# A reordered plan in a fused attention and token/channel mixer: five product tiles, a two-part split of the token result, and two more places for the token products

## The chip, the cores and the metric

The kernel runs on one core of one Trainium2 chip. The metric is the device time of one execution in microseconds (us). Engines are called as the profile calls them: PE (matrix products), PEld (its weight loads), DVE (vector), ACT (scalar), POOL (it issues the DMAs that accumulate) and SP (it issues most other DMAs).

## The reference

```python
def _attn_ref(x, weight_gen):                 # x: 8 x 4096 x 192, weight_gen: 8 x 4096 x 8 heads x 7
    w = softmax(weight_gen, axis=-1)
    out = np.einsum('bshk,bskhg->bshg', w, x_unf)   # 7 taps of the 6 rows before and the row itself
def _moe_ref(x, w_tok1, w_tok2, w_ch1, w_ch2):
    xt = x.transpose(0, 2, 1)
    h = np.maximum(xt @ w_tok1, 0.0) @ w_tok2       # over the 4096 tokens, 256 wide
    u = x + h.transpose(0, 2, 1)
    h2 = np.maximum(u @ w_ch1, 0.0) @ w_ch2         # over the 192 channels, 1536 wide
    return (u + h2).astype(np.float32)
```

The reference's weights are float64; the kernel receives them as such and turns each into float32 words on the chip ("conversion").

## The kernel before

The work is cut into 64 chunks of 512 tokens, `g` = 0 to 63, eight to a batch element. A prologue does the attention of the first eight chunks and their token-1 products. After it, one chunk of the main loop has four kinds of PE work:

- **channel 1** (`ph`, L573): six products of 18 matmuls, from the token result in two parts, `u_hi` and `u_lo`, each a single buffer;
- **channel 2** (`acc`, L591): six products `p` = 0 to 5 of 10 matmuls, from `h`, which ACT (L579) and DVE (L580) make of `ph` (four buffers of `h`). `p` = 4 and 5 read the last third of `w2s`;
- **token 2** (`up`, L524): 10 matmuls that give the token result of chunk g + 1. ACT first writes the residual into its bank (L518, the seed). Afterwards ACT and DVE copy the sum into `uf` (L531, L532, L536), and `u_parts` splits it: `u_hi` by L546 to L552 on ACT, `u_lo` by L548 and L549 on DVE and L553 to L555 on ACT;
- **token 1** (`th`, L507 in the first two batch elements, L490 and L492 later): adds one chunk of the next batch element into a running sum of eight. The eighth sum, through a relu, makes `h1`, without which token 2 of the next batch element can't start.

`ph`, `up` and `th` share three PSUM buffers in turn (`ps_w`). The fourth `ph` of a chunk so waits until the first has been read by L580, and the seed of an `up` that follows six `ph` waits for the fourth L580.

Beside this, DVE forms the attention of later chunks: 7 products (L211) and 3 additions (L225) for each chunk, two chunks at a time, through the tiles `pr` (four), whose sums POOL adds to `xa` by an accumulating DMA (L229). DVE and ACT also convert the rest of the weights (ACT L155 to L157, then DVE L159 to L161, then the split L166, L167), through `val` tiles of which three serve at a time. Token-1 weights of batch element 1 come back from DRAM into `val` tiles too (`load_w1`). At a chunk's end DVE turns the output (L645, L646, L648) and ACT copies it out in 12 pieces (L655).

What stands where on ACT and DVE is no fixed order. While the program is built, `pump` keeps a list of chains (attention, transposes, softmax, conversions, parts of u, stores) and a clock per engine of its own (`at`), and emits the next item of a chain when by that clock it fits before the next thing that PE needs. The constants near L677 (`SLACK_M`, `LATER` and so on) and the gates in the chains decide it. `picks` chooses whether token 1 or token 2 comes at the head of channel 2 or before `p` = 3. On the chip each engine then runs its list strictly in that order.

Of the kernel before, what the change touches and what calls it, by code (L numbers as in the profile page):

```python
# [12 lines left out]
F32 = mybir.dt.float32  # L13
# [8 lines left out]
def mixer_kernel(ctx: ExitStack, tc: tile.TileContext, x, wg, wt1, wt2, wc1, wc2, out):  # L22
    nc = tc.nc
    B, S, D = x.shape
# [20 lines left out]
    XA = 4  # L45
    PR = 4
    FT = NCH - 2
# [9 lines left out]

    ident = const.tile([P, P], F32, name="ident")
    make_identity(nc, ident)
    below = const.tile([P, 1], F32, name="below")  # L60
# [85 lines left out]
    def convert(raw, n, out):  # L146

        yield "gate", 0, lambda: state["vals"] < 2
        state["vals"] += 1
        v = val_tile()[:, 0:n]  # L150
        out.append(v)
        bits = v.bitcast(U32)
        low, high = raw[:, 0:n, 0], raw[:, 0:n, 1]
        act, stt = nc.scalar.activation, nc.vector.scalar_tensor_tensor
        yield "s", 950, lambda: act(v, high.bitcast(F32), AF.Abs)  # L155
        yield "s", 1050, lambda: act(v, v, AF.Sign, bias=below[:, 0:1])
        yield "s", 950, lambda: act(v, v, AF.Relu, scale=LOW30)  # L157
# [3 lines left out]
        yield "v", cost, lambda: stt(bits, high, 0xC0000000, bits, op0=ALU.bitwise_and, op1=ALU.bitwise_or)  # L161
# [98 lines left out]
    def two_parts(m):  # L260

        yield "gate", 0, lambda: state["token1"] >= m - 1

# [137 lines left out]
    def convert_w2(i):  # L401
        out = []
        yield from convert(rawt.pop(("w2", i)), KR * N, out)
        yield "n", 0, lambda: raw_free(tag_of["w2", i])
        yield "gate", 0, lambda: state["token2"] >= i - 1
        v, = out
        t = p1.tile([P, 2, KR * N], F32R, tag="w2", name="w2")
        yield from split(t[:, 0], t[:, 1], v)

        def last():  # L410
            state["vals"] -= 1
            w2t[i] = t
            nc.gpsimd.dma_start(s3[i], t.rearrange("p l n -> p (l n)").bitcast(F32))
        yield "n", 0, last
# [26 lines left out]
    def convert_channel(which, n, pool=None):  # L441
# [15 lines left out]
        def last():  # L457
            state["vals"] -= 1
            done.add((which, n))
        yield "n", 0, last  # L460
# [14 lines left out]
    def token1(m):  # L475
# [62 lines left out]
    def u_parts(m):  # L538
# [4 lines left out]
        f, act, dve = lo.bitcast(F32), nc.scalar.copy, nc.vector.tensor_sub  # L543
        yield "gate", 0, lambda: state["channel1"] >= m
        yield "w", 0, lambda: free["parts"]
        yield "u", 620, lambda: act(hi[:, 0], ua)  # L546
        yield "u", 620, lambda: act(hi[c, 2], uc[c])
        yield "v", 610, lambda: dve(lo[:, 0], ua, hi[:, 0].bitcast(F32))  # L548
        yield "v", 610, lambda: dve(lo[c, 2], uc[c], hi[c, 2].bitcast(F32))  # L549
        yield "u", 620, lambda: act(hi[c, 1], ua[e])  # L550
        yield "u", 620, lambda: act(hi[e, 1], ua[c])
        yield "u", 620, lambda: act(hi[e, 2], uc[c])  # L552
        yield "u", 620, lambda: act(lo[c, 1], f[e, 0])  # L553
        yield "u", 620, lambda: act(lo[e, 1], f[c, 0])  # L554
        yield "u", 620, lambda: act(lo[e, 2], f[c, 2])  # L555

        def last():
            ut[m] = hi, lo
            free["u"] = at["act"] + HOP
        yield "n", 0, last  # L560

# [134 lines left out]
    w_at, h1_at, h1s_at = deque([0.0] * 3), {0: 0.0}, [0.0]  # L696
    free = {"acc": 0.0, "u": 0.0, "t": 0.0, "parts": 0.0, "xh": 0.0}
    pr_free = deque([0.0] * PR)
# [87 lines left out]
    def next_lo():  # L786
# [7 lines left out]
             "summed": NCH - 1, "turned": FT - 1, "parts": NCH - 1, "kept": FT - 1, "stored": -1, "out": -1,  # L794
             "done": NCH - 1, "w1": NCH, "channel1": 0, "rest": 0}

# [53 lines left out]
    with tc.tile_pool(name="pro", bufs=1) as pro, \  # L850
            tc.tile_pool(name="ps_pro", bufs=1, space=bass.MemoryType.PSUM) as ps_pro:
        warm = pro.tile([P, 1], F32, name="warm")
        nc.scalar.activation(warm, ident[:, 0:1], AF.Exp)
# [7 lines left out]
        def start(items):  # L861

            items = iter(items)
            for _ in range(4):
                next(items)[2]()
            return items
# [73 lines left out]
    run(u_parts(0))  # L940
    free["u"] = 0.0
# [4 lines left out]
    at["dve"], at["act"] = 3500, 1500  # L946
    add_chain(load_w1(NCH))
    state["token2"] = 0

# [8 lines left out]
    def do_token1(it, m, t):  # L958
# [19 lines left out]
    def do_token2(it, m, t):  # L978
# [5 lines left out]
        w_at.append(t)  # L984
        chains.insert(3, Chain(u_parts(m), t, ("u", m)))
        state["token2"] = m
# [12 lines left out]
    def picks(g, soon, most):  # L999

        two = token2_ready(g + 1, soon)
        if two:
# [9 lines left out]
    for g in range(NG):  # L1012
        phs, kept = {}, {}
        soon = ((convert_w2, 1),) if g == 0 else ()
        for p in range(NP):
# [7 lines left out]
            if p < HB:  # L1023
                take_h(g, p, phs[p])
                w_at.append(on("dve", LOW, on("act", TOP, end)))
                if p == 0:
                    h_at = w_at[-1]
                if p == HB - 2:
# [10 lines left out]
        for p in range(NP):  # L1039
            if p == NP // 2:  # L1040
# [13 lines left out]
            on("pe", C2, free["acc"] if p == 0 else 0.0, h_at)  # L1054
            state["rest"] -= C2
            if p + HB < NP:
# [5 lines left out]
                take_h(g, p + HB, phs[p + HB])  # L1062
                h_at = on("dve", LOW, on("act", TOP, at["pe"]))
                if kept[p] in w_at:
                    w_at[w_at.index(kept[p])] = h_at
                if last:
                    picked += list(it)
                    h_at = 0.0
        pump(at["pe"] + SLACK_M)
# [45 lines left out]
```

## Time and profile before

| | |
|---|---|
| median of 3 runs | 2135.1 us (2129.74 to 2135.57) |
| the profiled execution | 2131.6 us, its span 2129.8 us |
| ACT busy | 68% of the span |
| POOL busy | 7% of the span |
| DMA moved | 363.82 MB, mean 171 GB/s |

A profile row of a group gives the line, engine, operation, the tiles, the count, then the busy time in us and the mean of one in ns, then the idle time of the engine before them with what ended it. A row of the timeline gives the start in us, the duration, the same names, and in brackets the idle time just before. A float32 product stands twice in the trace (16 rows for the 8 matmuls of a `th`).

### The profile page before, as it was taken

The page shows a single profiled execution, that of the slowest core. Times are in us where ns is not written, and L with a number is a line of the kernel's source. Part 1 is how long each engine was busy: PE and PEld are TensorE (multiplying, and loading weights), DVE is VectorE, ACT ScalarE, POOL GpSimd, SP SyncE. Part 2 cuts the span into 40 slices and gives each one's busy share as a digit, 9 for nine tenths or more (in the row PEclk, how much of TensorE's full clock was granted, in tenths as well). Part 3 has the DMA queues.
Part 4 walks back from the last instruction along what each step waited for, and adds up shares of the span by engine and source line. Part 5 has one row for each costly group of instructions (what it writes and reads, how often), then busy time and mean ns, then how long its engine had stood idle before and what let it go on. Part 6 is the DMA issues. An engine that isn't in the chain of part 4 may idle for free.

```text
span 2129.8 us, 32140 instructions
## 1 busy us (share of the span) xinstructions
PE 2085.4 (98%) x12766; PEld 1691.5 (79%) x12766; DVE 1538.5 (72%) x1760; ACT 1440.3 (68%) x2226; POOL 158.2 (7%) x194
## 2 busy tenths in 40 slices
PE   7989899999999999999999999999999999999998
PEld 5767788787878888888888888888888888888887
DVE  8978988788887777777777877777787765343433
ACT  5568666667766766676676677667666766766665
POOL 0001111000100010000000010000100000000000
PEclk9999999999999999999999999999999999999999
DMA  8666757878687667566766756676665655321221
GB/s 279 225 213 171 207 147 210 253 200 230 185 234 202 189 172 190 150 182 181 196 189 173 200 156 174 171 202 193 173 194 149 181 163 148 89 66 45 64 63 23
DMA packets 166198, 363.82 MB, mean 171 GB/s; under 512 B 16552, under 2 KB 105896, under 8 KB 150688
## 3 DMA queue, kind: packets, MB, share of 16 engines
q1 hardware_dynamic: 139808, 285.74, 42.8%
q0 software_dynamic: 25344, 74.46, 17.8%
q8 instruction: 100, 1.64, 0.3%
q10 hardware_dynamic: 896, 1.57, 0.2%
q14 instruction: 50, 0.41, 0.1%
HBM read 225.13 MB, written 70.52 MB: 139 GB/s over the span
## 4 chain that ended last, share of the span: by engine, by line
PE 82%; DVE 10%; ACT 4%; DMA 3%; issue 2%; POOL 0%; SPq 0%; ACTq 0%; DVEq 0%; POOLq 0%
PE acc L591 36%; PE ph L573 33%; PE up L524 7%; PE th L490 3%; DVE h L580 2%; DVE pr L211 2%; PE th L492 1%; DVE prk L327 1%; DMA raw<-in_moe_w_tok_dram 1%; PE th L507 1%; DMA xt<-in_x_dram 1%; DMA xa<-pr 1%; DVE val L160 1%; DVE val L159 1%; DVE pr L225 1%
## 5 line engine op out<-in xcount | busy, mean ns | idle before, releaser
L591 PE MATMUL acc<-h,w2s 128*128 128x512 f32 x3800 | 884.5, 390 | 2.5 <-DVE w2s L454 2.5
L591 PEld LDWEIGHTS acc<-h,w2s 128*128 128x128 f32 x3800 | 709.2, 188 | 148.9 <-DVE w2s L454 2.9
L579 ACT ACTIVATE h<-ph 128x1024 fp32r<-128x1024 f32 x384 | 394.4, 1027 | 396.2 <-PE ph L573 340.1
L580 DVE SCALAR_TENSOR_TENSOR h<-ph,h 128x1024 fp32r<-128x1024 f32 x384 | 467.1, 1217 | 121.3 <-ACT h L579 120.8
L573 PE MATMUL ph<-u_hi,w_hi 64*128 64x512 f32 x2304 | 343.5, 396 | 13.8 <-ACT u_hi L550 5.8
L573 PE MATMUL ph<-u_hi,w_lo 64*128 64x512 f32 x2304 | 332.9, 389 | 0.0
L573 PE MATMUL ph<-u_lo,w_hi 64*128 64x512 f32 x2304 | 332.4, 388 | 0.0
L211 DVE TENSOR_TENSOR pr<-xt,wg 128x768 f32<-128x768 f32 x336 | 314.0, 949 | 8.9 <-DMA xa<-pr 8.1
L573 PEld LDWEIGHTS ph<-u_hi,w_hi 64*128 64x128 f32 x2304 | 216.8, 185 | 82.8 <-issue 21.5
L573 PEld LDWEIGHTS ph<-u_hi,w_lo 64*128 64x128 f32 x2304 | 221.9, 185 | 47.3
L573 PEld LDWEIGHTS ph<-u_lo,w_hi 64*128 64x128 f32 x2304 | 221.8, 185 | 47.4 <-ACT u_lo L554 0.6
L229 POOL DMA_DIRECT2D xa<-pr x168 | 144.6, 861 | 1439.0 <-DVE pr L225 1236.9
L536 DVE TENSOR_TENSOR uf<-up,uf 64x512 f32<-64x512 f32 x63 | 43.0, 682 | 243.2 <-ACT uf L532 243.2
L655 ACT COPY out_tile<-oa 32x256 f32<-32x256 f32 x504 | 203.5, 404 | 7.8
L524 PE MATMUL up<-w,h 128*128 128x512 f32 x630 | 161.7, 402 | 5.9 <-ACT up L518 5.9
L225 DVE TENSOR_TENSOR pr<-pr 128x768 f32<-128x768 f32 x168 | 160.3, 954 | 3.7
L524 PEld LDWEIGHTS up<-w,h 128*128 128x128 f32 x630 | 113.8, 188 | 48.8 <-ACT up L518 16.2
L518 ACT COPY up<-xb 128x1024 f32<-128x1024 f32 x63 | 64.0, 1016 | 84.6 <-DVE h L580 81.5
L490 PE MATMUL th<-xh,w 128*128 128x384 f32 x384 | 112.5, 358 | 1.1 <-ACT th L483 1.1
L655 ACT COPY out_tile<-oc 32x256 f32<-32x256 f32 x252 | 101.6, 403 | 11.0 <-DVE oc L648 6.8
L269 DVE TENSOR_TENSOR xh<-xa,xh 128x768 fp32r<-128x768 f32 x48 | 45.9, 955 | 73.3 <-ACT xh L266 73.3
L492 PE MATMUL th<-xh,w 128*128 128x192 f32 x384 | 96.2, 250 | 0.0
(86 smaller groups left out, 1717.8 us busy)
## 6 DMA issues: line engine op xcount, KB each, us to landing
w<-s SPq DMA_DIRECT2D x96, 1024.0 KB, 5.3
xa<-pr POOLq DMA_DIRECT2D x168, 384.0 KB, 4.9
xt<-in_x_dram SPq DMA_DIRECT2D x56, 960.0 KB, 9.8
out_dram<-out_tile SPq DMA_DIRECT2D x128, 192.0 KB, 3.2
xs<-t SPq DMA_DIRECT2D x58, 384.0 KB, 4.6
xb<-xs SPq DMA_DIRECT2D x348, 64.0 KB, 5.0
raw<-in_moe_w_tok_dram SPq DMA_DIRECT2D x16, 1024.0 KB, 6.0
s<-w POOLq DMA_DIRECT2D x8, 1024.0 KB, 5.3
```

The lines of the kernel that those rows point to most:

```text
L211: nc.vector.tensor_mul(t.rearrange("p t (h g) -> p (t h) g", h=H).rearrange("p (o n) g -> p o n g", o=1), x_k, w)
L225: nc.vector.tensor_add(sums[m], sums[m], prt.pop(m))
L229: nc.gpsimd.dma_start(xat[m].rearrange("p t d -> p (t d)"), sums[m].rearrange("p t d -> p (t d)"), accum_op=ALU.add)
L490: nc.tensor.matmul(th[:, r, 0:2 * D], w[:, c, 0, rs], xh[:, c, :], start=i + c == 0, stop=False, skip_group_check=True)
L492: nc.tensor.matmul(th[:, r, 0:D], w[:, c, 1, rs], xh[:, c, 0:D], start=False, stop=c == CT - 1, skip_group_check=True)
L518: nc.scalar.copy(up.rearrange("p k (n b c) -> p (k n) c b", c=CT, b=Q), xb.rearrange("p k (n c b) -> p (k n) c b", c=CT, b=Q))
L524: nc.tensor.matmul(up[:, n, :], h1[:, k, d], w[:, l, k * N:(k + 1) * N], start=k == 0 and j == 0 and not seeded, stop=k == KR - 1 and j == ...
L573: nc.tensor.matmul(ph[:, j, :], w[rows, k, p * P:(p + 1) * P], u[rows, k], start=n == 0, stop=n == len(steps) - 1)
L579: nc.scalar.activation(h[:, :, 0, :], ph, AF.Relu)
L580: nc.vector.scalar_tensor_tensor(h[:, :, 1, :], ph, 0.0, h[:, :, 0, :].bitcast(F32), op0=ALU.max, op1=ALU.subtract)
L591: nc.tensor.matmul(acc[:, n, :], w2s[:, f, d], h[:, j, l, :], start=False, stop=f == NF - 1 and i == len(steps) - 1, skip_group_check=True)
L655: nc.scalar.copy(dst, src[to:to + Q].rearrange("p (n e d) -> p n e d", n=2, d=Q)[:, n])
```

## The change

`PR` becomes 5; `val` tiles become four after the prologue (with a wait in the plan's clock), and `ident` moves to the prologue's pool. The parts of u become two chains: one with the first two copies and all of `u_lo`, one with the three other copies of `u_hi`. Token-1 weights are fetched two chunks ahead from the start. The gate that let a chunk's sum count as ready only in turn goes for batch element 1. Channel 2 may have token 1 or token 2 also before its last product, and a token 1 that is behind (`ready[0][0] < g + NCH`, from g = 9) comes ahead of token 2 at its head. The wait for the last third of `w2s` moves in the plan from `p` = 3 to `p` = 4. Two matmuls of 128 columns are added at chunk 16's token 1. The plan keeps one due time per `h` and has other values of `LATER` and `SLACK_M`.

```diff
-    PR = 4
+    PR = 5
-        pool = pro if pro is not None and n % 6 >= 3 else p1
-        return pool.tile([P, NV], F32, tag="val", name="val", bufs=3)
+        pool = pro if pro is not None and n % 6 >= 4 else p1
+        return pool.tile([P, NV], F32, tag="val", name="val", bufs=2 if pool is pro else 4)
+        yield "w", 0, lambda: free["val"]
...
-        yield "gate", 0, lambda: state["token1"] >= m - 1
+        if m // NCH >= F1:
+            yield "gate", 0, lambda: state["token1"] >= m - 1
...
+                if m == F1 * NCH:
+                    nc.tensor.matmul(th[:, r, 2 * D:], w[:, CT - 1, 0, rs], xh[:, 0, 0:N - 2 * D],
+                                     start=False, stop=True, skip_group_check=True)
...
+        def first():
+            yield from begin()
+            yield "u", 620, lambda: act(hi[:, 0], ua)
+            yield "u", 620, lambda: act(hi[c, 2], uc[c])
+            yield "n", 0, lambda: taken.update(at=at["act"] + HOP)
+            yield "v", 610, lambda: dve(lo[:, 0], ua, hi[:, 0].bitcast(F32))
+            yield "v", 610, lambda: dve(lo[c, 2], uc[c], hi[c, 2].bitcast(F32))
+            yield "u", 620, lambda: act(lo[c, 1], f[e, 0])
+            yield "u", 620, lambda: act(lo[e, 1], f[c, 0])
+            yield "u", 620, lambda: act(lo[e, 2], f[c, 2])
+            yield "n", 0, last
+        def second():
+            yield from begin()
+            yield "gate", 0, lambda: "at" in taken
+            yield "u", 620, lambda: act(hi[c, 1], ua[e])
+            yield "u", 620, lambda: act(hi[e, 1], ua[c])
+            yield "u", 620, lambda: act(hi[e, 2], uc[c])
+            yield "n", 0, last
...
-    LATER = 5000
+    LATER = 4000
-    SLACK_M = 400
+    SLACK_M = 1000
...
+    add_chain(load_w1(NCH + 1))
-        while state["w1"] < min(m + 1 + (m >= F1 * NCH - 3), NG - 1):
+        while state["w1"] < min(m + 2, NG - 1):
-        chains.insert(3, Chain(u_parts(m), t, ("u", m)))
+        chains[3:3] = [Chain(items, t, ("u", m)) for items in u_parts(m)]
...
+        if most == 1 and g > NCH and ready and ready[0][0] < g + NCH and token1_ready(soon):
+            yield do_token1, begin_token1()
+            return
...
-                if g == 0:
-                    need(lambda: ("c2", 2) in done, (convert_channel, "c2", 2))
+            if g == 0 and p == 2 * NP // 3:
+                need(lambda: ("c2", 2) in done, (convert_channel, "c2", 2))
+            if p == NP - 1:
+                run_picked(picked)
...
+            if p == NP // 2 and token1_ready(C2) and ready[0][0] <= g + NCH:
+                picked = [(do_token1, begin_token1())]
+            if p == NP // 2 and not picked and token2_ready(g + 1, 2 * C2):
+                picked = [(do_token2, begin_token2(g + 1))]
```

Three places show what this does to the order. The first is ACT in chunk 0, from the split of a converted weight (L166) to the seed's successor and the last step (L157, now L156) of the conversion that gives the last third of `w2s`. Before:

```order
L166 CAST w2_867<-val_720 128x1024
L155 ACTIVATE val_884<-raw_714 128x768
L156 ACTIVATE val_884<-val_884,below_73 128x768
L518 COPY up_892<-xb1_79 128x8x4x32
L579 ACTIVATE h_894<-ph_831 128x2x512
L157 ACTIVATE val_884<-val_884 128x768
L155 ACTIVATE val_887<-raw_865 128x1024
L181 ACTIVATE wg_514<-wg_514 128x448
L531 COPY uf_672<-up_892 64x512
L532 COPY uf_672<-up_892 128x512
L453 CAST w2s_77<-val_884 128x4x192
```

And the same stretch now:

```order
L165 CAST w2_869<-val_722 128x1024
L523 COPY up_890<-xb1_74 128x8x4x32
L600 ACTIVATE h_892<-ph_833 128x2x512
L154 ACTIVATE val_886<-raw_714 128x768
L155 ACTIVATE val_886<-val_886,below_68 128x768
L180 ACTIVATE wg_514<-wg_514 128x448
L536 COPY uf_672<-up_890 64x512
L537 COPY uf_672<-up_890 128x512
L156 ACTIVATE val_886<-val_886 128x768
L454 CAST w2s_72<-val_886 128x4x192
```

The seed stands two steps earlier, and the last conversion step (L156 on `val_886`) behind the two copies that wait for `up`. Next on ACT, behind this, come the parts of u. Before:

```order
L546 CAST u_hi_925<-uf_672 128x512
L547 CAST u_hi_925<-uf_672 64x512
L156 ACTIVATE val_887<-val_887,below_73 128x1024
L157 ACTIVATE val_887<-val_887 128x1024
L155 ACTIVATE val_939<-raw_928 128x1024
L156 ACTIVATE val_939<-val_939,below_73 128x1024
L550 CAST u_hi_925<-uf_672 64x512
L551 CAST u_hi_925<-uf_672 64x512
L552 CAST u_hi_925<-uf_672 64x512
L553 CAST u_lo_926<-u_lo_926 64x512
```

And now:

```order
L564 CAST u_hi_924<-uf_672 128x512
L565 CAST u_hi_924<-uf_672 64x512
L577 CAST u_hi_924<-uf_672 64x512
L578 CAST u_hi_924<-uf_672 64x512
L579 CAST u_hi_924<-uf_672 64x512
L154 ACTIVATE val_887<-raw_867 128x1024
L155 ACTIVATE val_887<-val_887,below_68 128x1024
L156 ACTIVATE val_887<-val_887 128x1024
L154 ACTIVATE val_954<-raw_940 128x1024
L569 CAST u_lo_925<-u_lo_925 64x512
```

All five copies into `u_hi` now stand together, and the conversion steps stand between them and `u_lo`. The third place is PE in chunk 7, from its last `ph` to chunk 8's first. Before:

```order
L507 MATMUL th_2981<-xa_2116,val_2789 128x192 x8
L591 MATMUL acc_2911<-h_2855,w2s_77 128x512 x10
L591 MATMUL acc_2911<-h_2882,w2s_77 128x512 x10
L591 MATMUL acc_2911<-h_2908,w2s_77 128x512 x10
L507 MATMUL th_3053<-xa_2533,val_3007 128x192 x8
L591 MATMUL acc_2911<-h_2940,w2s_77 128x512 x10
L591 MATMUL acc_2911<-h_3032,w2s_77 128x512 x10
L591 MATMUL acc_2911<-h_3055,w2s_77 128x512 x10
L507 MATMUL th_3128<-xa_2535,val_3009 128x192 x8
L524 MATMUL up_3152<-w2_2708,h1_3145 128x512 x10
L573 MATMUL ph_3216<-u_hi_3177,w1_hi_75 128x512 x6
```

And now:

```order
L512 MATMUL th_2994<-xa_2599,val_2774 128x192 x8
L612 MATMUL acc_2924<-h_2870,w2s_72 128x512 x10
L612 MATMUL acc_2924<-h_2897,w2s_72 128x512 x10
L612 MATMUL acc_2924<-h_2921,w2s_72 128x512 x10
L512 MATMUL th_3061<-xa_2601,val_2828 128x192 x8
L612 MATMUL acc_2924<-h_2953,w2s_72 128x512 x10
L612 MATMUL acc_2924<-h_3046,w2s_72 128x512 x10
L529 MATMUL up_3107<-w2_2694,h1_3090 128x512 x10
L612 MATMUL acc_2924<-h_3063,w2s_72 128x512 x10
L594 MATMUL ph_3186<-u_hi_3142,w1_hi_70 128x512 x6
```

The batch element's last token 1 now has two channel-2 products between it and `up`, and `up` has one behind it; the third `th` of this chunk stands in an earlier one. Over the first nine chunks the number of `th` after each chunk's `ph` was 0, 0, 1, 1, 1, 1, 1, 3, 1 for g = 0 to 8 and is 0, 0, 1, 1, 2, 0, 2, 2, 0; from g = 9 it was one each and is 2, 0, 2, then one each. From g = 12 the sequence of PE's work is as before.

More of the change, by code (lines that the diff above doesn't have):

```diff
@@ L56, in mixer_kernel @@
     pro = None
-    ident = const.tile([P, P], F32, name="ident")
-    make_identity(nc, ident)
     below = const.tile([P, 1], F32, name="below")
@@ L411, in last @@
             state["vals"] -= 1
+            free["val"] = at["dve"] + HOP
             w2t[i] = t
@@ L458, in last @@
             state["vals"] -= 1
+            free["val"] = at["dve"] + HOP
             done.add((which, n))
@@ L543, in u_parts, with begin @@
         f, act, dve = lo.bitcast(F32), nc.scalar.copy, nc.vector.tensor_sub
[L544 to L555, printed above, removed]
-        def last():
-            ut[m] = hi, lo
-            free["u"] = at["act"] + HOP
-        yield "n", 0, last
+        left = [0, 1]
+        taken = {}
+        def begin():
+            yield "gate", 0, lambda: state["channel1"] >= m
+            yield "w", 0, lambda: free["parts"]
+        def last():
+            left.pop()
+            if not left:
+                ut[m] = hi, lo
+                free["u"] = at["act"] + HOP
+        def first():
[16 more added lines that the diff above has]
+            yield "n", 0, last
+        return first(), second()
     ht, acc_t = {}, {}
@@ L696, in mixer_kernel @@
     w_at, h1_at, h1s_at = deque([0.0] * 3), {0: 0.0}, [0.0]
-    free = {"acc": 0.0, "u": 0.0, "t": 0.0, "parts": 0.0, "xh": 0.0}
+    free = {"acc": 0.0, "u": 0.0, "val": 0.0, "t": 0.0, "parts": 0.0, "xh": 0.0}
     pr_free = deque([0.0] * PR)
@@ L794, in mixer_kernel @@
              "summed": NCH - 1, "turned": FT - 1, "parts": NCH - 1, "kept": FT - 1, "stored": -1, "out": -1,
-             "done": NCH - 1, "w1": NCH, "channel1": 0, "rest": 0}
+             "done": NCH - 1, "w1": NCH + 1, "channel1": 0, "rest": 0}
     def raw_free(tag):
@@ L851, in mixer_kernel @@
             tc.tile_pool(name="ps_pro", bufs=1, space=bass.MemoryType.PSUM) as ps_pro:
+        ident = pro.tile([P, P], F32, name="ident")
+        make_identity(nc, ident)
         warm = pro.tile([P, 1], F32, name="warm")
@@ L863, in start @@
             items = iter(items)
-            for _ in range(4):
+            for _ in range(5):
                 next(items)[2]()
@@ L939, in mixer_kernel @@
             nc.tensor.matmul(w[:, j, :], w1_hi[:, 0, 0:P], w1_hi[:, 0, 0:512], start=True, stop=True)
-    run(u_parts(0))
+    run(*u_parts(0))
     free["u"] = 0.0
@@ L1012, in mixer_kernel @@
     for g in range(NG):
-        phs, kept = {}, {}
+        phs, kept, h_at = {}, {}, {}
         soon = ((convert_w2, 1),) if g == 0 else ()
@@ L1048, in mixer_kernel @@
                 run_picked(picked)
-                if g == 0:
-                    need(lambda: ("c2", 2) in done, (convert_channel, "c2", 2))
             if g == NG - 1 and p == NP - HB:
                 break
+            if g == 0 and p == 2 * NP // 3:
+                need(lambda: ("c2", 2) in done, (convert_channel, "c2", 2))
+            if p == NP - 1:
+                run_picked(picked)
             channel2(g, p)
-            on("pe", C2, free["acc"] if p == 0 else 0.0, h_at)
+            on("pe", C2, free["acc"] if p == 0 else 0.0, h_at[p])
             state["rest"] -= C2
```

8 lines of the change are left out of this document (3 added, 5 removed).

## The prediction

> **What bounds the kernel now.** I read the page first, then the list of PE's waits, then the busy time by stretches, then the timeline around single waits.
>
> ```profile
> span 2129.8 us, 32140 instructions
> PE 2085.4 (98%) x12766; PEld 1691.5 (79%) x12766; DVE 1538.5 (72%) x1760; ACT 1440.3 (68%) x2226; POOL 158.2 (7%) x194
> ```
>
> PE is busy for 98% of the span: the order of the work can't win more than PE's idle time and what comes with it. A busy PE may still run slowly, so the stretches below are cut at starts of chunks (columns: stretch, its length, busy time of PE, PEld, DVE, ACT, POOL, then the granted clock, DMA share and rate):
>
> ```profile
> 159.25:192.20 32.95, 31.37 (x180) 24.15 (x179) 32.85 (x39) 27.03 (x40) 2.56 (x4) 0.95 0.57 165
> 192.20:227.28 35.08, 32.70 (x195) 25.80 (x194) 29.05 (x35) 30.10 (x45) 4.33 (x6) 1.00 0.70 197
> 227.28:266.43 39.15, 33.64 (x197) 27.30 (x196) 35.42 (x38) 23.89 (x37) 4.84 (x6) 0.96 0.69 200
> 266.43:360.32 93.89, 93.64 (x584) 77.04 (x584) 78.46 (x94) 62.06 (x100) 10.57 (x13) 1.00 0.69 183
> 360.32:401.41 41.09, 36.77 (x227) 30.86 (x226) 33.05 (x42) 22.81 (x40) 5.33 (x6) 1.00 0.76 207
> 401.41:436.68 35.27, 34.40 (x194) 27.55 (x194) 30.40 (x38) 23.38 (x34) 3.44 (x4) 0.90 0.91 256
> 436.68:630.05 193.37, 187.57 (x1167) 151.90 (x1166) 162.24 (x192) 134.68 (x208) 20.54 (x24) 1.00 0.77 217
> 630.05:1896.15 1266.10, 1266.10 (x7957) 1040.42 (x7956) 909.52 (x1068) 875.31 (x1370) 101.08 (x118) 1.00 0.63 171
> 288.24 2.60 PE th L507 x16
> ```
>
> The rows are chunks 1, 2, 3, then 4 to 6, 7, 8, 9 to 14, and 15 to 55; the last line, from the chain, is one float token 1. Chunks 15 to 55 have no idle time: 1266.10 / 41 = 30.9 us each, which is the floor of a chunk with one late token 1. Chunks 4 to 6 have one float token 1 each and 0.25 us of idle time: a floor of (93.89 - 0.25) / 3 = 31.2, and 31.2 - 2.6 = 28.6 without it. Over these floors chunk 1 loses 32.95 - 28.6 = 4.4, chunk 2 35.08 - 31.2 = 3.9, chunk 3 39.15 - 31.2 = 7.9, chunk 7 (three token 1) 41.09 - 36.4 = 4.7, chunk 8 35.27 - 30.9 = 4.4, chunks 9 to 14 193.37 - 6 x 30.9 = 8.0. That is 33 us, and the whole stake behind chunk 0: about 1.6% of the time.
>
> ```profile
> PE up L524 <- ACT up L518: 5.9, 11, 2.3
> PE ph L573 <- ACT u_hi L550: 5.8, 4, 2.0
> PE ph L573 <- DVE h L580: 5.5, 4, 3.1
> 154.47 4.85 PE L591 MATMUL acc<-h,w2s 128*128 128x512 f32 x20 [2.46 <-DVE w2s L454]
> 161.16 1.66 PE L573 MATMUL ph<-u_hi,w_hi 64*128 64x512 f32 x4 [1.41 <-ACT u_hi L550]
> 194.69 1.66 PE L573 MATMUL ph<-u_hi,w_hi 64*128 64x512 f32 x4 [1.99 <-ACT u_hi L550]
> 236.84 0.97 PE L573 MATMUL ph<-u_hi,w_hi 64*128 64x512 f32 x6 [3.12 <-DVE h L580]
> 255.06 4.55 PE L507 MATMUL th<-xa,val 128*128 128x192 f32 x16 [1.81 <-ACT th L483]
> 396.88 2.56 PE L524 MATMUL up<-w,h 128*128 128x512 f32 x10 [2.35 <-ACT up L518]
> 401.41 0.49 PE L573 MATMUL ph<-u_hi,w_hi 64*128 64x512 f32 x2 [1.97 <-ACT u_hi L546]
> 163.30:166.70 3.40, 3.40 (x18) 0.50 0.64 131
> 402.20:409.10 6.90, 6.33 (x27) 0.51 0.87 240
> 152.00:154.50 2.50, 0.04 (x2) 1.00 0.22 31
> ```
>
> These are three totals of PE's waits, the single waits of the early chunks, and three stretches of PE alone (length, busy, clock). PE waits for ACT and DVE work that stands too far back in its queue. Some waits cost twice: behind those at 161.16, 255.06 and 401.41 the clock is at half for 3.4, 3.4 and 6.9 us, so another 1.7, 1.7 and 3.4 us go without PE being idle. The wait at 154.47 left it at 1.00.
>
> **The change, term by term.** All terms are against the profiled execution, 2131.6 us (its span 2129.8); the three runs lie around it, their median 3.5 us above. The prologue and chunk 0 up to the seed keep their order: zero.
>
> *Chunks 0 and 1.* The rows of the last third of `w2s`:
>
> ```profile
> 146.12 1.01 ACT L518 COPY up<-xb 128x1024 f32<-128x1024 f32 x1
> 150.92 0.59 ACT L532 COPY uf<-up 128x512 f32<-128x512 f32 x1
> 152.15 0.94 DVE L161 SCALAR_TENSOR_TENSOR val<-raw,val 128x768 uint32<-128x768 uint32 x1
> 153.99 0.42 DVE L454 TENSOR_TENSOR w2s<-val,w2s 128x256 fp32r<-128x256 f32 x1 [0.90 <-ACT w2s L453]
> ```
>
> The seed moves ahead of two conversion steps (about 0.9 us each), so `up` loses only its 0.2 us of waiting, and ends near 149.3. But L157 (0.84) now stands behind L531 and L532 (0.6 each): it ends near 151.5; the three DVE steps (0.94 each), L453 (0.83) and L454 (0.42) follow, to 155.7, against 154.4. PE's wait of 2.46 becomes about 4. In return the copies of `u_hi` end 2 us before chunk 1 starts, and its wait of 1.41 goes. What is late next is `u_lo`: four conversion steps (1.15 each) now precede it on ACT, it is complete near 164.7, and the first `ph`, at 160.3, wants it after 1.4 us. That `ph` ends near 165, against 164.3 before, where half clock followed. I take zero, between -3 (half clock in both places) and +1.5.
>
> The Trainium skill (TensorE: Matmul & The Clock Gate, section Part 1: The HAM clock gate) says that activity is judged in free-running windows of about 3.4 us and that an idle window halves the clock. By it a wait of 4 us always costs one half window, an estimate of 1.7 us, and this term would be -1.7, the sum 16. The trace agrees that length alone doesn't decide (2.46 cost nothing, 1.41 did); it has no wait of 4 us.
>
> *Chunks 2 and 3.* They lose 11.8. In chunk 2 the five copies of `u_hi` again stand together behind `up` and end long before the chunk: the 1.99 goes. Chunk 3's wait of 3.12:
>
> ```profile
> 231.50 0.71 DVE L645 STREAM_TRANSPOSE oa<-acc 128x512 f32<-128x512 f32 x1
> 235.57 1.22 DVE L580 SCALAR_TENSOR_TENSOR h<-ph,h 128x1024 fp32r<-128x1024 f32 x1
> ```
>
> Chunk 3 starts at 227.28, the output turn only 4.2 us later, since two products of the next pair stand ahead of it; the first L580 starts 8.3 us in. Three `ph` take 6.2 us, so without a wait it must start by 5.0. In the changed order these products stand behind the fourth L580, one conversion step (1.2) lies between turn (2.1) and first L580, and it starts near 4.6; the fourth ends near 11.9 and its seed (1.0) comes 0.5 late. In chunk 2 an addition and two products (2.8) stand there: the first L580 starts near 5.5 and the seed is 0.9 late, 1.4 together. With 0.4 for small waits 11.8 becomes 2.3: +9.5. Bounds: +5, if DVE, busy for 97.3 of these 107.2 us (chunks 1 to 3), carries its debt on; +11.
>
> *Chunks 7 and 8.* They lose 9.1.
>
> ```profile
> 392.46 1.05 ACT L166 CAST w<-val 128x1024 fp32r<-128x1024 f32 x1 [6.25 <-DMA val<-s]
> 400.74 0.62 ACT L546 CAST u_hi<-uf 128x512 fp32r<-128x512 f32 x1
> 405.07 0.61 ACT L555 CAST u_lo<-u_lo 64x512 fp32r<-64x512 f32 x1
> ```
>
> The last token 1 now has two channel-2 products (4.5 us) before `up`; sum, relu and seed need 2.7, so the 2.35 goes. `up` has one product (2.3) behind it, and the way to L546's end takes 2.0, so the 1.97 goes too. What stays: from L546's start to the last `u_lo` 4.9 us, and a split L166 (1.05) now among them, 6.0. L546 starts 0.8 before the chunk, so `u_lo` is complete 5.2 us in, where 1.8 was wanted: 3.4 lost, and half clock (1.7) about two times in three. 9.1 becomes 4.5: +4.6. Bounds: +2, if L166, which still stands ahead of the sum, waits for its DMA as in the first row; +6.5.
>
> *Chunks 9 to 14.* They lose 8.0. DVE waits here for DMAs:
>
> ```profile
> 473.04 0.96 DVE L211 TENSOR_TENSOR xa<-xt,wg 128x768 f32<-128x768 f32 x1 [1.57 <-DMA xt<-in_x_dram]
> 501.47 0.96 DVE L211 TENSOR_TENSOR pr<-xt,wg 128x768 f32<-128x768 f32 x1 [2.41 <-DMA xa<-pr]
> 598.07 0.96 DVE L211 TENSOR_TENSOR pr<-xt,wg 128x768 f32<-128x768 f32 x1 [3.16 <-DMA xa<-pr]
> ```
>
> With four tiles in turn the first product of a group waits for the DMA two groups back; with five it is the second, one product (0.95) later, so each wait of the two lower rows loses that. Everything around them stands in another order, and no row says whether the waits meet PE again. Between 0 and +7.5 I take the middle, +4: less waiting, but the same DMAs. Chunks 4 to 6 stay at zero: at most two operations stand between turn and first L580.
>
> *The rest.* From chunk 15 on there is nothing to win. The two matmuls of 128 columns cost 0.3 at most by the columns. Fetching weights earlier, the gate and the moved buffers work on the plan alone.
>
> Sum: 0 + 9.5 + 4.6 + 4 - 0.3 = 17.8, and 2131.6 - 17.8 = **2114**.
>
> **The rivals.**
>
> *The waits only move.* The plan's clock isn't the chip's; DVE has no less to do. For it: DVE is busy 32.85 of 32.95 us in chunk 1, and two of my terms name a next wait. Against it: work does leave chunks 1 to 3. Half the middle terms: +7, 2125.
>
> *Everything goes.* All early losses to their bounds: 1.5 + 11 + 6.5 + 7.5 = 26.5, 2105. Against it: `u_lo` in chunk 8.
>
> *Nothing.* What the early chunks win, chunk 0's longer wait and chunks 9 to 14 give back: 2132.
>
> *Slower, from the even flow of chunks 15 to 55.* The 41 chunks without idle time have little room:
>
> ```profile
> 826.64 1.02 ACT L518 COPY up<-xb 128x1024 f32<-128x1024 f32 x1 [1.72 <-DVE h L580]
> 827.80 1.43 PE L524 MATMUL up<-w,h 128*128 128x512 f32 x5
> ```
>
> The seed ends 0.14 us before `up` starts. One more product ahead of the fourth L580 in each chunk would cost 0.81 x 41 = 33: 2147. It turns slower by 0.3% from 0.68 us a chunk. Against it: the changed order has at most as many attention operations there as before, in some chunks fewer, and the parts of u, though later, end 5 us before they are wanted.
>
> **How the numbers follow.** My forecast (2107 to 2121) 0.60, everything goes 0.08, the waits only move (2121 to 2129, partly under 0.3%) 0.19, nothing 0.06, slower 0.07. A measurement of this kernel tells about 0.3% (6.4 us) from no change. Faster 0.60 + 0.08 + 0.11 = 0.79; within it 0.08 + 0.06 = 0.14; slower 0.07. The range: the upper bounds sum to 2105, with 2 us for runs below the profile 2103; the lower, -3 + 5 + 2 + 0 - 0.3 = 3.7, give 2128, with 2 above it 2130.
>
> **What would show it.** Chunk 0's wait for L454 near 4 us, no wait for L550 in chunks 1 and 2, none over 1 us for L580 in chunk 3, no wait before chunk 8's `up` and 3 us inside its first `ph`; chunks 15 to 55 at 30.9. Wrong would make it: a wait for a DMA on ACT in chunk 7, or any idle time that returns in every chunk behind 15.

## The result, and the profile after

The changed kernel takes 2113.78 us (median of 4 runs, 2112.8 to 2114.38) against 2133.6; the ratio is 0.991, its 95% interval 0.9896 to 0.9924. The forecast was 2114. The time came out within a microsecond, but not all of the terms did. The forecast also counted 17.8 us from a profiled execution that ran 2.0 us below the median; by the medians the change won 19.8.

First the span and the list of PE's waits in the profile after (us in total, times, longest):

```profile
span 2111.0 us, 32145 instructions
PE acc L612 <- DVE w2s L455: 4.1, 1, 4.1
PE ph L594 <- DVE h L601: 3.4, 2, 1.8
PE ph L594 <- ACT u_hi L577: 2.4, 2, 1.6
PE up L529 <- ACT up L523: 2.1, 4, 0.6
```

Three single waits, from its timeline:

```profile
156.05 6.47 PE L612 MATMUL acc<-h,w2s 128*128 128x512 f32 x20 [4.05 <-DVE w2s L455]
389.13 0.49 PE L594 MATMUL ph<-u_hi,w_hi 64*128 64x512 f32 x1 [0.86 <-ACT u_hi L577]
678.42 0.96 PE L594 MATMUL ph<-u_hi,w_hi 64*128 64x512 f32 x6 [1.65 <-DVE h L601]
```

The three totals that carried the prediction (5.9, 5.8 and 5.5 us) are now 2.1, 2.4 and 3.4; the wait for `w2s` has grown. The stretches, with the columns as before:

```profile
12.10:162.40 150.30, 143.14 (x642) 103.66 (x642) 130.63 (x117) 92.30 (x116) 2.82 (x4) 0.98 0.71 239
162.40:193.80 31.40, 29.65 (x179) 23.05 (x178) 30.46 (x35) 28.13 (x42) 1.42 (x2) 1.00 0.46 146
193.80:226.10 32.30, 31.58 (x195) 25.63 (x194) 30.46 (x35) 27.75 (x41) 5.39 (x7) 1.00 0.80 215
226.10:257.40 31.30, 31.30 (x197) 25.75 (x196) 28.65 (x34) 22.71 (x35) 3.11 (x4) 1.00 0.65 191
257.40:353.90 96.50, 96.26 (x600) 79.66 (x599) 86.14 (x101) 64.87 (x104) 12.22 (x15) 1.00 0.72 203
353.90:387.80 33.90, 33.90 (x213) 28.33 (x212) 25.13 (x32) 18.57 (x30) 3.60 (x4) 1.00 0.73 213
387.80:420.10 32.30, 30.78 (x179) 23.35 (x180) 29.13 (x36) 25.32 (x40) 4.29 (x5) 1.00 0.83 230
420.10:607.90 187.80, 187.80 (x1185) 154.81 (x1184) 164.72 (x192) 135.97 (x209) 21.34 (x25) 1.00 0.77 213
607.90:703.80 95.90, 93.02 (x583) 76.00 (x582) 80.35 (x98) 64.57 (x101) 9.61 (x12) 1.00 0.75 212
703.80:1877.30 1173.50, 1173.50 (x7373) 964.39 (x7372) 836.78 (x980) 813.63 (x1270) 91.25 (x107) 1.00 0.62 171
```

The rows are the prologue with chunk 0, then chunks 1, 2, 3, 4 to 6, 7, 8, 9 to 14, 15 to 17, and 18 to 55 (30.9 each). Token 1 now stands in other chunks, so a stretch is compared after taking the moved ones (2.6 us each in the first two batch elements, 30.9 - 28.6 = 2.3 later) out:

| stretch | before | now | moved token 1 | won | predicted |
|---|---|---|---|---|---|
| chunks 0 and 1 (start of chunk 2) | 192.2 | 193.8 | none | -1.6 | 0 (-3 to +1.5) |
| chunks 2 and 3 | 74.2 | 63.6 | none | +10.6 | +9.5 (5 to 11) |
| chunks 4 to 6 | 93.9 | 96.5 | one more | 0 | 0 |
| chunks 7 and 8 | 76.4 | 66.2 | two fewer | +5.3 | +4.6 (2 to 6.5) |
| chunks 9 to 14 | 193.4 | 187.8 | one more | +7.9 | +4 (0 to 7.5) |
| chunks 15 to 17 | 3 x 30.9 = 92.7 | 95.9 | none | -3.2 | 0 |

The sum, 19.0 by these rounded numbers, is the difference of the spans, 2129.8 - 2111.0 = 18.8. Two terms missed by over 3 us in opposite directions.

### The profile page after: what moved, and what is told of

It reads as the page before. It is cut to its first block, busy times and chain, and to the rows that moved or that the text cites. A ratio compares the mean times of both kernels' runs of the same rounds, so it can differ in the third digit from the quotient of the medians.

```text
span 2111.0 us, 32145 instructions
## 1 busy us (share of the span) xinstructions
PE 2078.4 (98%) x12768; PEld 1688.9 (80%) x12768; DVE 1539.2 (73%) x1760; ACT 1444.7 (68%) x2226; POOL 157.7 (7%) x194
## 3 DMA queue, kind: packets, MB, share of 16 engines
q10 hardware_dynamic: 896, 1.57, 0.2%
## 4 chain that ended last, share of the span: by engine, by line
PE 94%; DVE 3%; ACT 1%; DMA 1%; issue 0%; POOL 0%; SPq 0%; ACTq 0%; DVEq 0%; POOLq 0%
PE acc L612 39%; PE ph L594 35%; PE up L529 7%; PE tapsum L338 4%; PE th L492 4%; PE th L512 2%; PE th L494 2%; DVE h L601 1%; DVE pr L210 1%; PE turn L348 1%; PE acc L629 0%; DMA xt<-in_x_dram 0%; DMA out_dram<-out_tile 0%; DVE pr L224 0%; ACT up L523 0%
## 5 line engine op out<-in xcount | busy, mean ns | idle before, releaser
L601 DVE SCALAR_TENSOR_TENSOR h<-ph,h 128x1024 fp32r<-128x1024 f32 x384 | 467.9, 1219 | 118.6 <-ACT h L600 117.8
L594 PE MATMUL ph<-u_hi,w_hi 64*128 64x512 f32 x2304 | 337.7, 394 | 6.3 <-DVE h L601 3.4
L594 PE MATMUL ph<-u_hi,w_lo 64*128 64x512 f32 x2304 | 328.5, 387 | 0.0
```

The costliest lines, as they stand in the source:

```text
L594: nc.tensor.matmul(ph[:, j, :], w[rows, k, p * P:(p + 1) * P], u[rows, k], start=n == 0, stop=n == len(steps) - 1)
L601: nc.vector.scalar_tensor_tensor(h[:, :, 1, :], ph, 0.0, h[:, :, 0, :].bitcast(F32), op0=ALU.max, op1=ALU.subtract)
```

## The experiments

Most of these keep every engine's order and alter one storage size, or keep all but one piece of one engine's order: the items of the plan and its clock are left alone, and only the instruction is issued earlier or later. Their line numbers are a few lines off those of the kernels they come from. The medians of the kernel before moved between 2132.3 and 2134.0 from one set of runs to the next, so a stage of the profile tells more than a difference of 1 us in the medians. Each kernel has one profile, and the same matmuls ahead of chunk 0's first `ph` start anywhere from 119.2 to 120.7 us in them, so stages are compared by their lengths.

**Four product tiles in the changed kernel's order.**

```diff
-            t = p1.tile([P, CT, D], F32, tag="pr", name="pr", bufs=PR)
+            t = p1.tile([P, CT, D], F32, tag="pr", name="pr", bufs=PR - 1)
```

> The changed kernel with every engine's order as it is, but four product tiles behind the five that the plan counts on. Theory (the tile itself): DVE's waits for the accumulating DMA, 8.1 us in four waits before the change and none now, come back, and since the plan now sets products earlier they are longer; chunks 9 to 14 lose 3 to 8 us again, chunks 2 to 8 at most 2: 2117 to 2124. Rival (the order alone won chunks 9 to 14): the waits come back on DVE but PE doesn't see them: 2113 to 2115.5.

It took 2115.55 us. DVE's waits for the accumulating DMA came back; that row of DVE's list of waits, before the change and here:

```profile
DVE pr L211 <- DMA xa<-pr: 8.1, 4, 3.2
DVE pr L210 <- DMA xa<-pr: 8.1, 9, 3.1
```

And chunks 9 to 14 among its stretches:

```profile
420.50:608.70 188.20, 188.04 (x1183) 154.66 (x1182) 164.81 (x192) 136.01 (x209) 21.39 (x25) 1.00 0.77 212
```

The stretch takes 188.2, only 0.4 more. In chunks 9 to 14 the rival was right. But the longest of the waits stands at the start of chunk 7, and there PE sees it (chunk 7, then rows of DVE and of PE):

```profile
352.40:387.80 35.40, 34.23 (x211) 28.22 (x210) 26.89 (x34) 18.39 (x30) 3.60 (x4) 1.00 0.69 204
353.05 0.96 DVE L210 TENSOR_TENSOR pr<-xt,wg 128x768 f32<-128x768 f32 x1 [3.05 <-DMA xa<-pr]
360.00 0.98 PE L594 MATMUL ph<-u_hi,w_hi 64*128 64x512 f32 x6 [1.17 <-DVE h L601]
```

Chunk 7 takes 35.4 in place of 33.9. Chunks 15 to 17 take 97.6 in place of 95.9, where DVE's wait for `xt` is 7.5 and not 6.7; that these 1.7 us are the tile's is not shown. Against this, the profile has no half clock in chunk 0's first `ph` and starts chunk 1 1.5 us earlier, so from there on it loses more than the 2.5 us between the two spans (2113.5 and 2111.0).

**Five product tiles in the order before.**

```diff
-            t = p1.tile([P, CT, D], F32, tag="pr", name="pr", bufs=PR)
+            t = p1.tile([P, CT, D], F32, tag="pr", name="pr", bufs=PR + 1)
```

> The kernel before with its order as it is, but five product tiles where its plan counts on four. Theory (the tile itself): DVE's waits for the accumulating DMA (8.1 us) fall under 1, its one wait for xt (1.6) stays; chunks 9 to 14, which lose 8.0 over their floor, win 3 to 6 of it, nothing else moves: 2127.5 to 2130.5. Rival (the order alone): under 1 us: 2132.5 to 2134.5.

It took 2130.0 us against 2134.0 (ratio 0.9983, 0.9974 to 0.9993). The DMA waits are gone, and chunks 9 to 14 take 189.5:

```profile
436.60:626.10 189.50, 186.52 (x1165) 151.89 (x1164) 162.09 (x192) 134.78 (x208) 20.48 (x24) 1.00 0.78 219
```

So the tile is worth 3.9 us there in the old order and 0.4 in the new, which needs it in chunk 7 instead (1.5). In the old order DVE's lateness in chunks 9 to 14 reaches PE; in the new it mostly doesn't.

**The later copies into u_hi held back to the first copy into u_lo.** In `u_parts` the three copies of the second chain are kept in a list, which the first `u_lo` copy empties:

```diff
-            yield "u", 620, lambda: act(lo[c, 1], f[e, 0])
+            yield "u", 620, lambda: (kept_back(), act(lo[c, 1], f[e, 0]))
...
-            yield "u", 620, lambda: act(hi[c, 1], ua[e])
+            yield "u", 620, lambda: copy(hi[c, 1], ua[e])
```

> The changed kernel with its order, but the three later copies into u_hi are issued only just ahead of the first copy into u_lo, as before the change. Theory (the split won chunk 1's and most of chunk 2's loss): in chunk 1 the third copy ends near 163.5 and the last u_lo near 166.6, where PE wants them from 162.9 and 163.9; the first ph there waits 2 to 3.5 us, chunk 2's 1.5 to 2.5, with or without half clock behind: 2117.5 to 2122, all of it in chunks 1, 2, 7 and 8. Rival (the copies end early enough in either place, and it was the other edits that emptied these chunks): under 1 us: 2113 to 2115. From chunk 15 on neither expects a change.

It took 2117.48 us, near the theory's range, but not in its chunks: chunks 1 to 3 took what they take in the changed kernel, and the loss lies in chunks 4, 8, 13 and 17 (1.2, 0.9, 1.3 and 1.9 us); its cause there is open. In chunk 1 (the timeline of ACT):

```profile
158.32 1.14 ACT L154 ACTIVATE val<-raw 128x1024 f32<-128x1024 f32 x1
159.48 1.78 ACT L559 CAST u_hi<-uf 64x512 fp32r<-64x512 f32 x3
161.29 0.62 ACT L579 CAST u_lo<-u_lo 64x512 fp32r<-64x512 f32 x1
```

The three copies end at 161.3, and chunk 1 starts at 161.6: its late start, behind the wait for `w2s`, covers them. My 163.5 forgot that the steps ahead of them move up by the copies' 1.8 us. So the split alone did not empty chunks 1 and 2; whether it would matter in chunk 1 without that late start was not tried.

**The last third of w2s earlier in chunk 0.** Of that conversion alone, L156 and the three DVE steps are issued with L155's item:

```diff
-        yield "s", 1050, lambda: act(v, v, AF.Sign, bias=below[:, 0:1])
+        yield "s", 1050, lambda: (act(v, v, AF.Sign, bias=below[:, 0:1]), joined and [f() for f in steps])
...
-        yield from convert(rawt.pop((which, n)), NF2 * D if which == "c2" else HF, out)
+        yield from convert(rawt.pop((which, n)), NF2 * D if which == "c2" else HF, out, (which, n) == ("c2", 2))
```

> The changed kernel with one piece of chunk 0 earlier: the last conversion step of the last third of w2s (L156) directly behind the step ahead of it on ACT, and its three DVE steps ahead of the sum of up. By the rows of the profile after: L156 ends at 149.3, the DVE steps at 152.3, L454 at 153.2, L455 at 154.1: PE's wait of 4.05 becomes 2.1. Theory 1 (the half-clock stretch of 3.4 us behind it comes of the long wait): it goes too, and chunk 2 starts 3.5 us earlier: 2110. Theory 2 (the stretch comes either way): 2 us: 2112. Rival (the time is given back in chunk 1, since u_lo and the first h come no earlier against PE): 2113 to 2115.

It took 2109.18 us. The wait is 1.91, and chunk 1 starts at 157.8 in place of 162.4:

```profile
153.03 4.86 PE L615 MATMUL acc<-h,w2s 128*128 128x512 f32 x20 [1.91 <-DVE w2s L458]
```

Of PE alone, the stretch behind the wait in the changed kernel:

```profile
157.00:160.40 3.40, 3.40 (x10) 0.50 1.03 375
```

And here:

```profile
153.00:157.80 4.80, 4.77 (x20) 1.00 0.99 329
```

The half clock went with the long wait: theory 1. About 0.8 of the 4.6 us is another stretch of half clock, in chunk 0's first `ph` (last section), that this profile doesn't have; the run with both moves has it and starts chunk 1 at 158.6.

**Four val tiles in the order before.**

```diff
-        return pool.tile([P, NV], F32, tag="val", name="val", bufs=3)
+        return pool.tile([P, NV], F32, tag="val", name="val", bufs=3 if pool is pro else 4)
```

> The kernel before with its order as it is, but four val tiles after the prologue in place of three. In chunk 1 of before ACT stood 2.16 us at a conversion step (L155, 191.68) until DVE's L167 gave a val tile back, and the copies into u_hi for which PE then waited 1.99 us stood behind that step; ACT's waits of this kind are 4.2 us in three places. Theory (the tile is what held chunk 2's copies): ACT's wait goes, PE's wait of 1.99 at the start of chunk 2 goes, chunks 2 and 3 (74.2 us) become 71 to 72.5: 2130.5 to 2132.5. Rival (the order is, since the steps still stand ahead of the copies): under 0.7 us: 2133.3 to 2134.5.

It took 2128.43 us against 2133.93. The row of ACT's waits for a `val` tile before (`ACT val L155 <- DVE w L167: 4.2, 3, 2.2`) is gone from the list. Chunks 2 and 3 take 33.0 + 36.5 = 69.5 in place of 74.2, more than expected: chunk 2's 1.99 is gone, and of chunk 3's waits the one for token 1 fell from 1.81 to 0.41. Chunk 4 gives 1.0 of the 4.7 back (32.2 in place of 31.2), with a wait of 0.73 for L580.

```profile
193.40:226.40 33.00, 32.53 (x195) 26.02 (x194) 29.53 (x36) 28.00 (x43) 4.40 (x6) 1.00 0.75 208
226.40:262.90 36.50, 33.49 (x197) 26.79 (x196) 33.26 (x37) 23.62 (x36) 4.83 (x6) 0.95 0.71 211
```

**All storage of the change, in the order before.** Both edits above, with two `val` tiles and `ident` in the prologue's pool:

```diff
-    ident = const.tile([P, P], F32, name="ident")
+        ident = pro.tile([P, P], F32, name="ident")
...
-        pool = pro if pro is not None and n % 6 >= 3 else p1
-        return pool.tile([P, NV], F32, tag="val", name="val", bufs=3)
+        pool = pro if pro is not None and n % 6 >= 4 else p1
+        return pool.tile([P, NV], F32, tag="val", name="val", bufs=2 if pool is pro else 4)
```

> The kernel before with its order as it is and all of the changed kernel's storage: five product tiles, four val tiles, ident in the prologue's pool. Alone, the product tile won 4.0 and the val tile 5.5 us. Theory (they act in different places, chunks 9 to 14 and chunk 2 to 3): 9 to 10 us together: 2124 to 2125.5, and the order alone brings the other half of the change's 20. Rival (one hides the other, since what DVE gets done earlier waits at the next DMA): 2127 to 2129.

It took 2125.37 us against 2132.94 (ratio 0.9964, 0.995 to 0.9978). The two gains stand side by side, 69.4 in chunks 2 and 3 (chunk 4 again gives 1.0 back) and 189.4 in chunks 9 to 14:

```profile
194.20:263.60 69.40, 65.93 (x391) 52.90 (x390) 62.77 (x72) 51.53 (x79) 9.13 (x12) 0.98 0.73 210
435.00:624.40 189.40, 186.61 (x1165) 151.91 (x1164) 162.12 (x192) 134.76 (x208) 20.48 (x24) 1.00 0.79 222
```

Storage alone, in the old order, is 7.6 us of the change's 20, and the other order on top of it the rest. The new order with three `val` tiles was not run, so what that tile is worth there is open.

**Chunk 3's products behind its fourth L580, in the kernel before.** From the last `h` of chunk 2 on, attention's instructions go to a list that is emptied behind that L580:

```diff
+    def emit(f):
+        held.append(f) if state.get("hold") else f()
...
-            nc.vector.tensor_add(sums[m], sums[m], prt.pop(m))
+            emit(lambda: nc.vector.tensor_add(sums[m], sums[m], prt.pop(m)))
```

> The kernel before with one piece of DVE's order altered: the four products and the addition of the next pair that stood ahead of and among the first four L580 of chunk 3 are issued behind the fourth. Theory (they held back the first L580, and PE with it): the first L580 starts 5.8 us into the chunk and not 8.3, PE's wait of 3.12 becomes 0.6; chunk 3 wins 2.5, and up to 3.5 more where the wait of 1.81 and the stretch of half clock behind it go too: 2128 to 2131.5. Rival (the products are only late elsewhere, and DVE, busy all through chunks 1 to 3, gives the time back at the next seed): under 1 us: 2133 to 2134.5.

It took 2131.88 us against 2132.94 (ratio 0.9995, 0.9987 to 1.0004): no change. Its waits in chunk 3, from the timeline:

```profile
233.78 0.96 PE L607 MATMUL ph<-u_hi,w_hi 64*128 64x512 f32 x6 [0.66 <-DVE h L614]
254.29 4.83 PE L519 MATMUL th<-xa,val 128*128 128x192 f32 x16 [4.79 <-ACT th L492]
```

The first wait fell from 3.12 to 0.66, and the second rose from 1.81 to 4.79: the rival, though the time was given back at token 1 and not at a seed. Chunk 3 takes 39.2 either way.

**The same products held back into chunk 4.** As above, but six pieces stay behind all through chunk 3, and the rest follows the fourth L580 of chunk 4:

```diff
+                if g == 4 and p == HB - 1:
+                    state["lag"] = 0
+                    flush()
...
+                state["lag"] = 6 if g == 2 and last or g == 3 else 0
```

> The kernel before with the order of PE, ACT and SP as it is; on DVE (and in the accumulating DMAs) the attention of one pair of chunks stands up to six pieces later all through chunk 3, and what is left of it is issued behind the fourth L580 of chunk 4. So chunk 3 not only has no products ahead of its first L580 (which alone brought nothing: PE's wait for L580 fell from 3.12 to 0.66 and its wait for token 1 rose from 1.81 to 4.79), but has 14 pieces in place of 18 up to the next output turn, 3.8 us less for DVE. Theory (what bound chunks 1 to 3 is DVE's load, 97.3 us of 107.2, and only work that leaves them shortens them, as the change's order does with 89.5 us): both waits go, chunk 3 takes 33 to 35 us in place of 39.2, chunk 4 gives at most 1 back: 2127 to 2130. Rival (the load isn't it; chunk 3 is held by ACT's conversion steps and the copies behind them): chunk 3 stays over 38: 2131.5 to 2134.

It took 2128.79 us against 2132.27 (ratio 0.9988, 0.9979 to 0.9997). Chunk 3:

```profile
227.30:263.20 35.90, 33.45 (x195) 27.19 (x194) 32.03 (x34) 23.86 (x37) 3.99 (x5) 0.95 0.62 189
```

And its wait for token 1, from the timeline:

```profile
251.91 4.55 PE L526 MATMUL th<-xa,val 128*128 128x192 f32 x16 [1.80 <-ACT th L499]
```

It takes 35.9, with DVE busy for 32.0 and not 35.4, and chunk 4 gives nothing back. That is between theory and rival: the gain of the first wait now stays, because the work left the chunk, but the wait for token 1 is what it was.

**Chunk 7's token 2 behind the last product again.**

```diff
             if p == NP - 1:
+                if g == NCH - 1:
+                    channel2(g, p)
                 run_picked(picked)
-            channel2(g, p)
+            if g != NCH - 1 or p < NP - 1:
+                channel2(g, p)
```

> The changed kernel with PE's order altered at one place: in chunk 7 token 2 stands behind the last product of channel 2, as before the change, not ahead of it. Theory (the product is the cover of the way from up to u_hi and u_lo): up ends 2.3 us later against chunk 8, whose first ph waits 2.3 us for the first copy and still 1.4 for the later ones, with a stretch of half clock or without: chunks 7 and 8 take 68.3 to 70.5 in place of 66.2: 2115.8 to 2118.5. Rival (token 1's new place alone won there, since PE loses the same time at u_lo either way): under 0.7 us: 2113 to 2114.5.

It took 2115.72 us, and chunks 7 and 8 took 68.7 in place of 66.2: the theory. The wait for the first copy, from the timeline:

```profile
390.54 0.50 PE L594 MATMUL ph<-u_hi,w_hi 64*128 64x512 f32 x2 [2.25 <-ACT u_hi L564]
```

**The x loads of chunks 28 and 29 ahead of six gathers on SP.**

```diff
+        if m == 19 and not behind_x:
+            behind_x.append(m)
+            return
...
+        if m == 28:
+            load_xt(19)
```

> The changed kernel with one thing moved: on SP the two loads of the x tiles of chunks 28 and 29 stand ahead of six gathers of xb, not behind them. In the profile after they were issued at 663.5 (the first gather at 657.0), and DVE, which had reached their first product at 661.4, stood 6.7 us; chunks 15 to 17 took 95.9 us, 3.3 over before. Theory (the queue's order makes them late): they land 6 us earlier, DVE waits under 1 us, chunks 15 to 17 take 92.6 to 93.2: 2110 to 2111.5. Rival (the DMA engines were busy, and the loads land late wherever they stand): at most 1 us: 2112.8 to 2114.5.

It took 2111.86 us. The same pair's loads and first product in the kernel before (SPq rows give the time of the issue):

```profile
658.10 2.83 SPq L94 DMA_DIRECT2D xt<-in_x_dram  x2
677.92 0.94 DVE L211 TENSOR_TENSOR xa<-xt,wg 128x768 f32<-128x768 f32 x1
```

In the changed kernel:

```profile
657.02 4.61 SPq L315 DMA_DIRECT2D xb<-xs  x6
663.52 0.83 SPq L92 DMA_DIRECT2D xt<-in_x_dram  x2
668.18 0.96 DVE L210 TENSOR_TENSOR xa<-xt,wg 128x768 f32<-128x768 f32 x1 [6.74 <-DMA xt<-in_x_dram]
```

And of this one:

```profile
657.92 1.31 SPq L92 DMA_DIRECT2D xt<-in_x_dram  x2
667.02 0.96 DVE L210 TENSOR_TENSOR xa<-xt,wg 128x768 f32<-128x768 f32 x1 [4.74 <-DMA xt<-in_x_dram]
```

Chunks 15 to 17:

```profile
608.70:702.70 94.00, 92.85 (x585) 76.12 (x584) 80.48 (x98) 64.71 (x101) 9.68 (x12) 1.00 0.77 217
```

Neither was wholly right: they take 94.0 in place of 95.9. The loads were issued 5.6 us earlier and served DVE only 1.2 us earlier by the clock of the trace (this run is 0.8 later at chunk 15). But PE's wait of 1.65 at chunk 17 went. Two waits of PE for a seed, 0.6 us each, stay.

**Both moves.** The edits of chunk 0 and of the x loads together.

> The changed kernel with both moves, that of chunk 0's conversion steps (alone 2109.2) and that of the x loads ahead of the gathers. If the two places are independent: 2109.2 - 3.3 = 2105.5 to 2106.5. If the gain of the first was in part a matter of where the clock's stretches fall, it can differ by 1.5 us a stretch: up to 2109.

It took 2106.74 us against 2133.93 (ratio 0.987, 0.9857 to 0.9884), the best of all: 7 us under the changed kernel. By the two gains alone (4.6 and 1.9) it would be 2107.3.

## Why the prediction was right, and where it was not

**Chunks 0 and 1: the steps were right, the size was off.** The wait for L455 is 4.05 (forecast about 4) and L577's wait in chunk 1 is gone. I took zero, on the ground that half clock would move from chunk 1 to nowhere; it came behind the 4.05, and chunk 2 starts 1.6 later. Of this 0.4 was there ahead of chunk 0's first `ph` (a product ahead of it starts at 119.92 and not 119.48), so the term itself is nearer -1.2. By the clock-gate rule of the Trainium skill (TensorE: Matmul & The Clock Gate, section Part 1: The HAM clock gate) this term was -1.7; the trace agrees with the half clock, and the term lies nearer to that than to zero. A new wait of 1.75 for L601 in chunk 1 had no step of its own.

**Chunks 2 and 3: the sum was right, the reason was not.** The waits went, and chunk 3's first L601 starts at 230.01, 3.9 us into the chunk, where I said 4.6. But I put the 9.5 us down to where copies and products stand. The runs show that moving the products alone wins nothing, since DVE's debt turns up at the next wait, and holding the copies back costs nothing there. What they show to win, both in the old order, is a fourth `val` tile (4.7 us, less the 1.0 in chunk 4) and work that leaves DVE (3.3 us of chunk 3 for 3.4 us of work). The change does both: DVE was busy for 97.3 us in chunks 1 to 3 and is now for 30.46 + 30.46 + 28.65 = 89.6. That work left stood in the prediction only as an argument against a rival. How the 10.6 split in the new order between the tile, less work on DVE and token 1's later place in chunk 2 was not tried.

**Chunks 7 and 8: right.** `up` and its successors no longer make PE wait before chunk 8; putting one product back costs 2.5 us, where I had counted 2.0. Token 1's new place was not tried alone. What stays in chunk 8, 32.3 - 28.6 = 3.7, has the forecast size (3.4) without half clock, which I had put at two times in three.

**Chunks 9 to 14: too small by 4.** All idle time went (187.80 of 187.80), beyond the upper bound of 7.5. I took the middle of 0 to 7.5 because the same DMAs stay. The runs with four and five tiles show that the fifth tile alone is worth 3.9 in the old order, and that the new order hardly needs it in these chunks. That DVE's waits for DMAs could stay and still not reach PE was not in the term. Which piece of the order took them off PE's path is open.

**Chunks 15 to 17: the term that was missing.** I wrote that from chunk 15 on there is nothing to win, and gave no thought to a loss: the sequence of PE is as before, but DVE reaches the products of chunks 28 and 29 before their tiles have landed and stands 6.74 us. It isn't DVE that is early: it is ready at 661.4, 53.5 us behind the start of chunk 15, and before the change it came there after 47.9 (677.92 - 630.0). The loads are late: they go out 55.6 us behind that start (663.52 - 607.9), where it was 28.1 (658.10 - 630.0). DVE ends the pair before, whose two tiles they take over, 45.5 us behind it and not 29.8, and six gathers then stand ahead of them. PE's waits in the stretch:

```profile
PE ph L594 <- DVE h L601: 1.6, 1, 1.6
PE up L529 <- ACT up L523: 1.2, 2, 0.6
```

So the loads account for 1.6 to 1.9 of the 3.2; the two seeds, which stay with the loads moved, are most of the rest. DVE's wait is of the kind named in the prediction's last part, in another place and on another engine; it comes once, not in every chunk.

So the mechanism was right for chunks 7 and 8 and for the steps of chunk 0, and not for chunks 2 and 3. That the time came out at 2114 was in part luck: two terms were wrong by +3.9 and -3.2, which nearly cancel, and a base 2.0 us below the median made up for a gain that by the medians was forecast 2.0 too small.

## What to carry to other kernels

A wait that goes may come back as the next wait when the engine waited for is busy nearly all the time: move work out of the full stretch, not only out of the way. To tell storage from order in a planned kernel, give the plan one number of buffers and the pool another. And where instructions move, compare the place of each DMA in its queue with the instruction that needs it, past the stretch that the change was about.

## What the runs showed of the hardware

The stretch of half clock depends on more than the wait ahead of it. Chunk 0's first `ph` waits 1.58 us in the changed kernel and 1.57 in the run with the earlier third of `w2s`; the 3.4 us behind it, PE alone, in the first:

```profile
126.30:129.70 3.40, 3.31 (x15) 0.50 0.10 28
```

And in the second:

```profile
126.30:129.70 3.40, 3.21 (x23) 1.00 0.11 31
```

And the wait of 4.05 was followed by 3.4 us at half clock in the changed kernel, and had 6.8 us of it around its end in the run that holds the copies back:

```profile
152.60:159.40 6.80, 4.83 (x11) 0.50 0.77 245
154.57 7.09 PE L622 MATMUL acc<-h,w2s 128*128 128x512 f32 x20 [4.05 <-DVE w2s L455]
```

In the changed kernel the two stretches start 30.7 us apart, nine times 3.41 us, which is the length that the trace records for one; in the profile before, those at 163.3 and 402.2 start 238.9 us apart, 70 times that. The Trainium skill (TensorE: Matmul & The Clock Gate, section Part 1: The HAM clock gate) calls the window free-running, which these rows agree with. That an idle window halves the clock, as the prediction has it from there, does not cover the stretch behind 1.58 us, ahead of which PE was busy for 1.75 of 3.40 us (122.9 to 126.3). A wait of 4.05 was followed by half clock in all five runs that have it. As to the price, the 20 matmuls behind that wait take 6.47 and 7.09 us with half clock and 4.86 without, and from chunk 0's first `ph` to the end of the wait it is 30.06 us with the early stretch (125.99 to 156.05) and 29.33 without (125.27 to 154.60, the run with four product tiles). So one stretch is worth 0.7 to 1.6 us here, and the early one comes and goes in runs whose edits lie elsewhere.
